# One instruction for the masked products, and an identity matmul for the own-step part, in an RWKV attention with a mixer behind it

## The chip, the cores and the metric

The kernel runs on one core of one Trainium2 chip. The metric is the device time of one execution in microseconds; of several runs the median is given. Engines are named as in the profile: PE is TensorE, DVE is VectorE, ACT is ScalarE, POOL is GpSimd, SP is SyncE, which here only issues DMAs.

## The reference

An RWKV recurrence with decay w and a bonus u for the own step, over batch 4, 8 heads, 768 steps, head size 48, and behind it a mixer over tokens (768 to 256 to 768) and channels (384 to 1536 to 384):

```python
for t in range(S):
    kt, vt, rt = (k[:, :, t], v[:, :, t], r[:, :, t])
    cur = np.einsum('bhd,bhe->bhde', u[None] * kt, vt)
    y[:, :, t] = np.einsum('bhd,bhde->bhe', rt, state + cur)
    state = w[None, :, :, None] * state + np.einsum('bhd,bhe->bhde', kt, vt)
...
h = np.maximum(xt @ w_tok1, 0.0) @ w_tok2
u = x + h.transpose(0, 2, 1)
h2 = np.maximum(u @ w_ch1, 0.0) @ w_ch2
return (u + h2).astype(np.float32)
```

Everything arrives and leaves as float32; the kernel computes most products in bf16.

## The kernel before

The 768 steps are cut into C = 6 chunks of 128, so a batch has six units (b, c), and there are 24. Inside a unit the recurrence becomes matmuls. k and r are scaled by powers of the decay (kp, rp, or wpT behind the transpose); A = kp rT, with steps that aren't earlier masked out, is multiplied with v; the state of the chunks before comes in through a matmul with S0; and the own step, u times k times r summed over a head, times v, is added. Heads lie in pairs of 64 partitions (two times 48, padded), HP = 4 pairs, and q = 0 or 1 tells which of a pair.

A unit goes through four stages, one slot apart, and each slot s runs each stage for another unit (the list STAGES in `slot`):

- `stage_p`: kp (on DVE for batch 0 but units 3 and 5, else on POOL); for batch 0 also m = k*r on POOL, for later batches rp and ku on POOL.
- `stage_a`: transposes on PE through the PSUM pool psM (four buffers, tag "m"). For batch 0 trk, trr and mT, in f32 but for trk, which ACT copies out but for trr, which DVE multiplies with wpT into rk. ACT casts v to vb.
- `stage_b`: eight matmuls give A in two PSUM tiles at_ps0 and at_ps1, one for each q; DVE multiplies each with the mask into AT0 and AT1 (bf16). For batch 0 the own step's sums come from three f32 matmuls with u_blk (ad_ps) and a copy on ACT (adg); for later batches DVE has made adg in stage_a.
- `stage_c`: y_ps sums the state's part, then A times v; kv_ps holds the state, which ACT copies out, or DVE behind chunk 2 (times wGm). DVE adds y_ps and yd, and writes x_b, the mixer's input.

yd = vb times adg is made by `own_step` on POOL: in stage_c for batch 0, in stage_b for the others.

Every engine runs its instructions in the order of the program text, so an instruction that waits holds all behind it on its engine. Batch 0 runs alone (slots 0 to 8, with one or two idle matmuls on PE behind the stages of slots 0 to 5). At the end of slots 4 to 7 POOL issues the DMAs of the mixer's weights, which also cast them to bf16: WEIGHTS_AT says which (wtok_194 in slot 4, wtok_195 in 5, wch_0 in 6, wch_1 and wch_198 in 7). At the end of slots 0 and 1 POOL makes powers, at the end of slot 3 wGm. SP issues the input loads of all units in order; that of batch 1's first unit waits, by a dependency written by hand, for the last x_b of batch 0 (`after[1, 0] = done[0, C - 1]`). From there PE's list of mixer matmuls for one batch (`up`: z_ps, `down`: h_ps) is interleaved with the slots of the next batch's attention by `merge`, which works from costs and due times written by hand.

Of the kernel before, what the change touches and what calls it, by code (L numbers as in the profile page):

```python
# [11 lines left out]
f32 = mybir.dt.float32  # L12
bf16 = mybir.dt.bfloat16
# [9 lines left out]
def kernel(  # L23
# [14 lines left out]
    B, H, S, D = r.shape  # L38
    dm = H * D
    T = 128  # L40
# [3 lines left out]
    HP = H // 2  # L44
# [8 lines left out]
    apool = ctx.enter_context(tc.tile_pool(name="apool", bufs=3))  # L53
# [3 lines left out]
    psA = ctx.enter_context(tc.tile_pool(name="psA", bufs=1, space=bass.MemoryType.PSUM))  # L57
# [12 lines left out]
    pe, dve, act, pool, sp = (InOrder(e) for e in (nc.tensor, nc.vector, nc.scalar, nc.gpsimd, nc.sync))  # L70

    def h3(t):
        return t.rearrange("p (h d) -> p h d", h=H)
# [3 lines left out]
    done = {}  # L77
# [62 lines left out]
    ident_f = const.tile([128, 128], f32, name="ident_f")  # L140
# [5 lines left out]
    mask = const.tile([128, 128], f32, name="mask")  # L146
# [99 lines left out]
    x_bs = [xpool.tile([128, C, dm], bf16, name="x_b", bufs=3) for b in range(B)]  # L246
# [63 lines left out]
    def own_step(L):  # L310
        L["yd"] = apool.tile([128, dm], f32, name="yd")
        pool.tensor_mul(h3(L["yd"]), h3(L["vb"]), L["adg"].unsqueeze(2).to_broadcast([128, H, D]))

    def stage_b(b, c):

        L = live[b, c]
        rk = L["rk"]
        if b > 0:
            own_step(L)
        at_ps = [psA.tile([128, HP, T], f32, name=f"at_ps{q}", tag=f"at{q}") for q in range(2)]  # L320
        for a in range(HP):
            for q in range(2):
                rows = slice(q * P, q * P + D)
                pe.matmul(at_ps[q][:, a, :], rk[rows, 0, a, :], rk[rows, 1, a, :], start=True, stop=True)
        L["AT"] = []
        for q in range(2):
            AT = apool.tile([128, HP, T], bf16, name=f"AT{q}")
            dve.tensor_mul(AT, at_ps[q], mask.unsqueeze(1).to_broadcast([128, HP, T]))
            L["AT"].append(AT)
        if b == 0:  # L330

            ad_ps = psM.tile([128, H], f32, name="ad_ps", tag="m")
            for j in range(3):
                pe.matmul(ad_ps, L["mT"][:, j, :], u_blk[:, j, :], start=(j == 0), stop=(j == 2))
            L["adg"] = apool.tile([128, H], f32, name="adg")
            act.copy(L["adg"], ad_ps)

    state = {}

    def stage_c(b, c):  # L340
        L = live.pop((b, c))
        rk, kp, vb = L["rk"], L["kp"], L["vb"]
        if b == 0:
            own_step(L)
        S0 = state.pop(b, None)
        y_ps = psA.tile([128, dm], f32, name="y_ps", tag="y")
        first = True
        if c > 0:
            for a in range(HP):
                pe.matmul(y_ps[:, ds(a * 2 * D, 2 * D)], rk[:, 1, a, :],  # L350
                   S0[:, a].rearrange("p q d -> p (q d)"),
                   start=first, stop=False, skip_group_check=True)
                first = False
        if c < C - 1:

            if c % G == 0:
                kv[0] = psA.tile([128, HP, 2, D], f32, name="kv_ps", tag="kv")
                if c > 0:
                    pe.matmul(kv[0].rearrange("p a q d -> p (a q d)"), ident,
                       S0.rearrange("p a q d -> p (a q d)"),  # L360
                       start=True, stop=False, skip_group_check=True)
            for a in range(HP):
                pe.matmul(kv[0][:, a].rearrange("p q d -> p (q d)"),
                   kp[:, 2 * a:2 * a + 2, :].rearrange("p q d -> p (q d)"),
                   vb[:, ds(a * 2 * D, 2 * D)],
                   start=(c == 0 and a == 0), stop=True, skip_group_check=True)
        for a in range(HP):
            for q in range(2):
                h = 2 * a + q
                pe.matmul(y_ps[:, ds(h * D, D)], L["AT"][q][:, a, :], vb[:, ds(h * D, D)],  # L370
                   start=first, stop=(h == H - 1), skip_group_check=True)
                first = False
        if c < C - 1:
            if c % G != G - 1:
                new = S0s[c % G]
                for q in range(2):
                    rows = slice(q * P, q * P + D)
                    act.copy(new[rows, :, q, :], kv[0][rows, :, q, :])
            else:
                new = apool.tile([128, HP, 2, D], bf16, name="S0")  # L380
                dve.tensor_mul(new, kv[0], wGm)
            state[b] = new
        done[b, c] = dve.tensor_add(x_bs[b][:, c, :], y_ps, L["yd"])


    mixed = {}
# [65 lines left out]

    units = [(b, c) for b in range(B) for c in range(C)]
    STAGES = ((3, stage_c), (2, stage_b), (1, stage_a), (0, stage_p))

    def slot(s, lo, hi):

        for lag, f in STAGES:
            if lo <= s - lag < hi:
                f(*units[s - lag])  # L460

# [10 lines left out]
    for s in range(C + 3):  # L472
        slot(s, 0, C)
        if s < C:
            keep_warm(WARM[1 if s < 4 else 2])
        if s < 2:
            decay_k(s + 1)
            exponents(s + 1)
        if s == 0:
            constants_1()  # L480
        if s == 3:
            constants_2()
        if 0 < s < 3:
            decay_rT(s)
        if s == 8:
            constants_3()
        if 4 < s < 8:
            decay_r(s - 5)
        load_weights(WEIGHTS_AT.get(s, ()))
        if s == C - 1:  # L490
            sp.dma_start(u_bc, u.rearrange("h d -> (h d)").partition_broadcast(128))
        if s == C + 1:
            for f in hid[:3]:
                f()
# [26 lines left out]
    def att(t, s):  # L521
        return (t, SLOT, lambda: slot(s, C, len(units)))
# [29 lines left out]
    for b in range(1, B):  # L552
# [4 lines left out]
        if b + 1 < B:  # L557
            at = [1.0, 5.0, 9.0, 13.0, 17.0, 21.5, 26.0, 30.5] if b == 1 else [0.0, 6.0, 12.0, 18.0]
# [35 lines left out]
```

## Time and profile before

| | |
|---|---|
| median of 3 runs | 186.15 us (186.05 to 186.49) |
| span of the profiled execution | 184.1 us |
| busy: PE, PEld, DVE, ACT, POOL | 165.5, 106.8, 106.0, 100.0, 93.8 us |
| chain that ended last: PE, POOL, DMA, DVE, ACT | 58%, 14%, 13%, 6%, 5% |
| DMA | 24.44 MB in 90354 packets, 133 GB/s over the span |

The span runs from the first to the last instruction of the profiled execution. What lies around it is in the runs' time and not in the span; the profiled execution has no other time of its own here, so the median stands beside the span, 2.05 us above it. PEld is the loading of weights into TensorE, which overlaps its matmuls. The chain is followed back from the last instruction to what released each one; it names what set the end, which busy time does not. All the kernel's operations go through one helper and so have one line, L68, in the profile: they are told apart by the names of their tiles.

### The profile page before, as it was taken

The numbers are of one execution on the slowest core, as the hardware profiler recorded it, in microseconds if no ns is written. First come the engines' busy times: TensorE is split into PE (matmuls) and PEld (weight loads), VectorE is DVE, ScalarE is ACT, GpSimd is POOL, SyncE is SP. The second block draws the span as 40 slices with busy tenths as digits, with TensorE's granted clock in tenths as the row PEclk, the third lists the DMA queues.
The fourth block names the chain that finished last, engine by engine and source line by source line (L and its number), as shares of the span: only waits on it lengthen the run. The fifth ranks groups of instructions, "written<-read, shape, count | busy, mean of one in ns | idle before, by whom it ended". The sixth has DMA issues, their size and how long they took to land.

```text
span 184.1 us, 3991 instructions
## 1 busy us (share of the span) xinstructions
PE 165.5 (90%) x1504; PEld 106.8 (58%) x1504; DVE 106.0 (58%) x193; ACT 100.0 (54%) x217; POOL 93.8 (51%) x113
## 2 busy tenths in 40 slices
PE   7788888893699899798999999899999999999992
PEld 2376776461367566465667666666665665656651
DVE  6465877700469999974669977996541071121121
ACT  2695565493578744404959748654645444445500
POOL 5459795002999999943597999991100000000000
PEclk9999999999699999999999999999999999999999
DMA  4999998999999998124699999233011134211212
GB/s 92 185 203 163 191 141 143 196 184 196 187 219 215 234 225 195 45 45 107 136 235 232 189 243 196 44 67 108 0 46 43 43 86 89 85 43 43 85 47 85
DMA packets 90354, 24.44 MB, mean 133 GB/s; under 512 B 83680, under 2 KB 90336, under 8 KB 90336
## 3 DMA queue, kind: packets, MB, share of 16 engines
q1 hardware_dynamic: 86368, 20.85, 54.0%
q0 software_dynamic: 3408, 3.15, 11.0%
q10 hardware_dynamic: 560, 0.20, 0.7%
q8 instruction: 12, 0.20, 0.4%
q14 instruction: 6, 0.05, 0.1%
HBM read 20.84 MB, written 4.72 MB: 139 GB/s over the span
## 4 chain that ended last, share of the span: by engine, by line
PE 58%; POOL 14%; DMA 13%; DVE 6%; ACT 5%; issue 3%; ACTq 0%; SPq 0%; DVEq 0%; POOLq 0%
PE h_ps L68 23%; PE z_ps L68 20%; DMA rt<-in_r_dram 8%; POOL ku L68 3%; POOL yd L68 3%; DMA wd<-in_w_dram 3%; PE tr_ps L68 3%; DMA uT<-u_sb 3%; PE y_ps L68 2%; PE ad_ps L68 2%; POOL rp_661 L68 2%; POOL rp_663 L68 1%; PE hT_ps L68 1%; POOL rp_665 L68 1%; DVE u_sb L68 1%
## 5 line engine op out<-in xcount | busy, mean ns | idle before, releaser
L68 ACT ACTIVATE zr<-z_ps 128x384 bf16<-128x384 f32 x96 | 44.3, 495 | 31.7 <-PE z_ps L68 31.6
L68 PE MATMUL h_ps<-wch_198,zr 128*128 128x384 bf16 x288 | 50.4, 326 | 0.2
L68 PEld LDWEIGHTS <-zr 128*128 128x128 bf16 x288 | 28.0, 98 | 18.9 <-issue 1.0
L68 DVE TENSOR_TENSOR osb<-u_sb,h_ps 128x384 f32<-128x384 bf16 x24 | 13.3, 552 | 44.5 <-PE h_ps L68 44.5
L68 ACT COPY rk<-tr_ps 128x1024 bf16<-128x1024 bf16 x18 | 18.2, 1012 | 19.2 <-PE tr_ps L68 18.7
L68 PE MATMUL z_ps<-uT,wch_0_196 128*128 128x384 bf16 x144 | 27.6, 337 | 1.1 <-DMA uT<-u_sb 1.1
L68 PE MATMUL z_ps<-uT,wch_1_197 128*128 128x384 bf16 x144 | 26.5, 326 | 0.8 <-ACT zr L68 0.6
L68 DVE TENSOR_TENSOR rku<-ku,rt 128x384 f32<-128x384 f32 x18 | 18.6, 1033 | 11.3 <-POOL ku L68 11.3
L68 POOL TENSOR_TENSOR yd<-vb,adg 128x384 f32<-128x384 bf16 x24 | 20.0, 834 | 7.3 <-DVE adg L68 6.7
L68 PEld LDWEIGHTS <-wch_0_196 128*128 128x128 bf16 x144 | 14.0, 101 | 10.4 <-issue 3.2
L68 POOL TENSOR_TENSOR ku<-kt,u_bc 128x384 f32<-128x384 f32 x18 | 20.0, 1110 | 0.0
L68 PEld LDWEIGHTS <-wch_1_197 128*128 128x128 bf16 x144 | 13.8, 98 | 10.1 <-issue 1.7
L68 DVE TENSOR_TENSOR x_b<-y_ps,yd 128x384 bf16<-128x384 f32 x24 | 13.3, 553 | 10.6 <-POOL yd L68 5.6
L68 POOL TENSOR_TENSOR kp_139<-kt,wn 128x384 bf16<-128x384 f32 x7 | 7.0, 999 | 17.2 <-DMA kt<-in_k_dram 11.5
L68 PEld LDWEIGHTS <-rk 48*128 48x128 bf16 (+1 forms) x272 | 11.4, 95 | 6.3 <-issue 3.0
L68 DVE TENSOR_TENSOR u_sb<-x_b,hT_ps 128x384 bf16<-128x384 bf16 x24 | 11.8, 547 | 1.5 <-PE hT_ps L68 1.5
L68 ACT CAST vb<-vt 128x384 bf16<-128x384 f32 x24 | 12.3, 514 | 0.0
L68 DVE TENSOR_REDUCE adg<-rku 128x8 f32<-128x384 f32 x18 | 9.9, 553 | 0.8
L68 PE MATMUL hT_ps<-h1r,wtok_195 128*128 128x384 bf16 x48 | 9.4, 326 | 0.9 <-ACT h1r L68 0.8
L68 PE MATMUL idle_ps<-warm 128*128 128x512 bf16 x20 | 7.8, 520 | 2.2 <-DVE warm L68 1.3
L68 PE MATMUL h_ps<-x_b,wtok_194 128*128 128x384 bf16 x48 | 8.9, 325 | 0.1
L68 POOL TENSOR_TENSOR rp_661<-rt,wp 128x384 bf16<-128x384 f32 x6 | 6.6, 1101 | 3.1 <-DMA rt<-in_r_dram 3.1
(318 smaller groups left out, 253.6 us busy)
## 6 DMA issues: line engine op xcount, KB each, us to landing
kt<-in_k_dram SPq DMA_DIRECT2D x24, 192.0 KB, 3.7
vt<-in_v_dram SPq DMA_DIRECT2D x24, 192.0 KB, 3.9
out_dram<-osb SPq DMA_DIRECT2D x24, 192.0 KB, 1.9
rt<-in_r_dram SPq DMA_DIRECT2D x18, 192.0 KB, 3.9
wch_198<-in_moe_w_ch_dram POOLq DMA_DIRECT2D x1, 1152.0 KB, 17.6
wch_0_196<-in_moe_w_ch_dram POOLq DMA_DIRECT2D x1, 576.0 KB, 8.9
wch_1_197<-in_moe_w_ch_dram POOLq DMA_DIRECT2D x1, 576.0 KB, 10.5
wtok_194<-in_moe_w_tok_dram POOLq DMA_DIRECT2D x1, 384.0 KB, 7.5
```

The costliest lines, as they stand in the source:

```text
L68: return lambda *args, **kw: tc.keep_in_program_order(f(*args, **kw))
```

## The change

Three things change, all in the attention.

- The two PSUM tiles at_ps0 and at_ps1 become one of the same size in total, which spans two banks, and DVE multiplies it with the mask in one instruction of 1024 elements a partition. This holds for all 24 units.
- In chunks 0 to 3 of batch 0 a last matmul, with the f32 identity as weights and yd as moving operand, adds the own-step part to y_ps, and ACT copies y_ps to x_b. In the other 20 units DVE adds as before. In batch 0 `own_step` moves from stage_c to the end of stage_b.
- In batch 0's slots the order of the stages becomes c, p, b, a, where it was c, b, a, p.

On the engines this gives the following order. POOL has yd of a unit ahead of what ends the slot (wGm and the weight DMAs) where it had it behind. DVE has kp ahead of a slot's mask product and rk. PE has one more f32 matmul in four slots, ahead of the next unit's at_ps. ACT has one more copy in these slots, ahead of adg.

```diff
         if b > 0:
             own_step(L)
-        at_ps = [psA.tile([128, HP, T], f32, name=f"at_ps{q}", tag=f"at{q}") for q in range(2)]
+        at_ps = psA.tile([128, 2, HP, T], f32, name="at_ps", tag="at")
         for a in range(HP):
             for q in range(2):
                 rows = slice(q * P, q * P + D)
-                pe.matmul(at_ps[q][:, a, :], rk[rows, 0, a, :], rk[rows, 1, a, :], start=True, stop=True)
-        L["AT"] = []
-        for q in range(2):
-            AT = apool.tile([128, HP, T], bf16, name=f"AT{q}")
-            dve.tensor_mul(AT, at_ps[q], mask.unsqueeze(1).to_broadcast([128, HP, T]))
-            L["AT"].append(AT)
+                pe.matmul(at_ps[:, q, a, :], rk[rows, 0, a, :], rk[rows, 1, a, :], start=True, stop=True)
+        AT = L["AT"] = apool.tile([128, 2 * HP, T], bf16, name="AT")
+        dve.tensor_mul(AT, at_ps.rearrange("p q a t -> p (q a) t"),
+                       mask.unsqueeze(1).to_broadcast([128, 2 * HP, T]))
         if b == 0:
...
             act.copy(L["adg"], ad_ps)
-
+            own_step(L)
+
+    BY_PE = 4
     state = {}
...
-        if b == 0:
-            own_step(L)
+        add_by_pe = b == 0 and c < BY_PE
...
-                pe.matmul(y_ps[:, ds(h * D, D)], L["AT"][q][:, a, :], vb[:, ds(h * D, D)],
-                   start=first, stop=(h == H - 1), skip_group_check=True)
+                pe.matmul(y_ps[:, ds(h * D, D)], L["AT"][:, q * HP + a, :], vb[:, ds(h * D, D)],
+                   start=first, stop=(h == H - 1 and not add_by_pe), skip_group_check=True)
                 first = False
+        if add_by_pe:
+            pe.matmul(y_ps, ident_f, L["yd"], start=False, stop=True, skip_group_check=True)
...
-        done[b, c] = dve.tensor_add(x_bs[b][:, c, :], y_ps, L["yd"])
+        if add_by_pe:
+            done[b, c] = act.copy(x_bs[b][:, c, :], y_ps)
+        else:
+            done[b, c] = dve.tensor_add(x_bs[b][:, c, :], y_ps, L["yd"])
...
+    STAGES0 = ((3, stage_c), (0, stage_p), (2, stage_b), (1, stage_a))
+
     def slot(s, lo, hi):
 
-        for lag, f in STAGES:
+        for lag, f in (STAGES if lo else STAGES0):
```

## The prediction

> **What bounds the kernel now.** I read the page first, then the chain of waits in order of time, then busy time by stretches, the timeline around 14 to 33 us, and the DMA view of single stretches. The page gives the span and the chain's shares:
>
> ```profile
> span 184.1 us, 3991 instructions
> PE 58%; POOL 14%; DMA 13%; DVE 6%; ACT 5%; issue 3%; ACTq 0%; SPq 0%; DVEq 0%; POOLq 0%
> ```
>
> One page row can't place a change that touches mostly the first 32 us, so the chain in order of time comes next (start, length, what):
>
> ```profile
> 31.19 0.56 DVE x_b L68
> ...
> 32.19 14.15 DMA rt<-in_r_dram
> 46.48 1.00 POOL rp_661 L68
> ...
> 73.23 1.28 POOL rp_663 L68
> 74.55 0.40 PE tr_ps L68 x4
> ```
>
> So there are four stages. Batch 0's attention ends with the last x_b at 31.75. The loads of batch 1 wait for that x_b by hand. Then one input row, rt of unit (1,0), is under way until 46.3. Then POOL runs until PE takes over. The stretches say which of them has slack (busy time of PE, PEld, DVE, ACT, POOL, then clock, DMA share, GB/s):
>
> ```profile
> 31.75:46.48 14.73, 10.53 (x72) 5.94 (x71) 4.19 (x10) 8.26 (x19) 1.00 (x2) 1.00 1.20 192
> 46.48:74.55 28.07, 25.18 (x285) 16.88 (x286) 23.96 (x36) 17.40 (x34) 28.07 (x29) 0.94 1.00 207
> 84.43:184.10 99.67, 95.01 (x826) 60.48 (x826) 48.82 (x86) 52.94 (x112) 36.38 (x37) 1.00 0.43 102
> ```
>
> POOL has no gap in 28.07 us: whatever moves its start at 46.48 moves all that follows. Ahead of it the DMA engines are full (share 1.20), so the start is set by bytes and by when they are queued. The last 100 us are PE's, and the change takes nothing from PE there.
>
> **The change part by part. Mask product in one instruction.** Two instructions of 512 elements become one of 1024:
>
> ```profile
> 15.36 0.68 DVE AT_346 L68
> 16.04 0.60 DVE AT_348 L68
> ...
> 16.69 0.20 PE L68 MATMUL y_ps<-vb,AT_348 128*128 128x48 bf16 x1 [0.40 <-DVE AT_348 L68]
> ```
>
> A pair takes 1.28 us. x_b, with 384 elements, takes 0.56 (above) and a half product, with 512, 0.68: 0.12 for 128 elements, so 512 more cost 0.50 and the merged one 1.18, a gain of 0.10 a unit; at worst it takes twice 0.68, a loss of 0.08. The chain holds DVE for 6% of the span, mostly ahead of 32 us; behind it I count 0.1 us of gain in all. The Trainium skill ("Perfetto Trace Analysis", Optimizing Scalar/DVE Operations) says against it that an engine that is not saturated but makes others wait should have its instructions broken up. The last row shows how little that is here: the y products alternate between the halves, so only one of eight started early, and PE then waited 0.40 for the second half. By that rule a unit would lose that one product's head start, by the row nothing.
>
> **Own-step part by TensorE, four units.** It removes four x_b additions (0.56 each) from DVE, and with them DVE's wait for POOL's yd:
>
> ```profile
> 14.03 0.82 POOL L68 TENSOR_TENSOR yd<-vb,adg 128x384 f32<-128x384 bf16 x1
> 14.88 0.56 DVE L68 TENSOR_TENSOR x_b<-y_ps,yd 128x384 bf16<-128x384 f32 x1 [1.76 <-POOL yd L68]
> ```
>
> The wait isn't gone, it changes engine: the identity matmul waits for the same yd, and behind it in PE's queue stand the next unit's at_ps, ad_ps and transposes, which ran during DVE's wait before. yd of unit 0 still stands on POOL right behind m of unit 2, so PE is held until 14.87. From there PE's work for a slot is, by the chain:
>
> ```profile
> 12.61 0.17 PE kv_ps L68 x4
> 12.78 0.20 PE y_ps L68 x8
> 12.98 0.16 PE at_ps_336 L68
> ...
> 17.29 0.21 PE at_ps_408 L68
> ...
> 17.69 0.77 PE ad_ps L68 x6
> 18.45 0.24 PE trk L68 x4
> 18.69 0.45 PE trr L68 x4
> 19.14 0.33 PE mT_ps L68 x3
> 19.46 0.23 PE idle_ps L68
> ...
> 28.56 0.21 PE at_ps_614 L68
> ...
> 29.72 0.99 PE h_ps L68 x6
> ```
>
> From at_ps to the end of idle 2.40 (17.29 to 19.69), the state's products about 0.17 (taken like kv_ps), kv_ps 0.17, y_ps 0.20: 2.94. The identity matmul (128x384, f32) is in no row. An f32 matmul is recorded twice (ad_ps x6 for three); trr, f32 with 128 columns, takes 0.45/4 = 0.11, so 384 columns 0.34, twice: 0.68. At least it is two passes at the bf16 pace (h_ps, 384 columns: 0.99/6 = 0.165), 0.33; at most each pass costs double the transposes' pace, 1.36. I take 0.68, the nearest row in type. A slot is then 3.62, and at_ps starts: unit 1 at 14.87 + 0.68 = 15.55 (at_ps_336 at 12.98 before); unit 2 at 19.37 (0.20 for a second idle matmul); unit 3 at 22.99; unit 4 at 26.78 (0.17 for a carried state). Unit 5, with no identity matmul between, at 29.72, against 28.56. Its x_b ended 3.19 behind that (31.75 - 28.56): 32.9. Batch 0 ends about 1.2 us later. DVE, eased by some 0.66 a slot, is no longer what PE waits for: a merged product that starts 0.5 behind at_ps is done 1.7 behind it, and PE needs it 2.7 behind.
>
> ScalarE gets four copies, near this one of the same size:
>
> ```profile
> L68 ACT COPY mT<-mT_ps 128x384 f32<-128x384 f32 x6 | 2.9, 478 | 1.1 <-PE mT_ps L68 1.1
> ```
>
> Each 0.48 us stands ahead of adg, which waits for ad_ps 1.1 us behind the identity matmul: hidden; if it weren't, adg and yd would come up to 0.48 later.
>
> **Order of the stages.** Putting stage_p ahead of b and a makes DVE do kp of unit 1 before rk of unit 0 (0.55 us) and kp of unit 2 before the first mask product. at_ps of unit 0 comes about 0.5 later, its mask product about 1.5; both end ahead of 14.87, when PE is held by yd anyway, so nothing. Without that hold the product's delay would count.
>
> **own_step moved to stage b.** On POOL it goes past what ends a slot: wGm and the weight DMAs. Those now stand behind a yd that waits for a fresh adg:
>
> ```profile
> 26.06 0.80 POOL L68 DMA_DIRECT2D wch_0_196<-in_moe_w_ch_dram  x1
> ...
> 27.66 0.80 POOL L68 DMA_DIRECT2D wch_1_197<-in_moe_w_ch_dram  x1
> 28.46 1.05 POOL L68 DMA_DIRECT2D wch_198<-in_moe_w_ch_dram  x1
> 30.06 0.83 POOL L68 TENSOR_TENSOR yd<-vb,adg 128x384 f32<-128x384 bf16 x1 [0.56 <-ACT adg L68]
> 31.78 0.37 SPq L68 DMA_DIRECT2D kt<-in_k_dram  x1
> ```
>
> The last yd started 1.50 behind its at_ps (30.06 - 28.56). So yd of unit 4 starts at 26.78 + 1.50 = 28.28 and ends 0.83 later: wch_0 is issued at 29.1, 3.0 later. yd of unit 5 ends at 32.05: wch_1 and wch_198 are issued at 32.05 and 32.85, 4.4 later. The inputs of batch 1 are issued at 32.9 instead of 31.78. What this costs, the DMA view of two stretches tells, 28 to 30 and 36 to 42 (queue, packets, MB, share of 16 engines):
>
> ```profile
> DMA packets 180, 0.26 MB, mean 131 GB/s; under 512 B 14, under 2 KB 179, under 8 KB 179
> ...
> q0 software_dynamic: 179, 0.25, 81.2%
> ...
> DMA packets 2226, 1.11 MB, mean 185 GB/s; under 512 B 1120, under 2 KB 2226, under 8 KB 2226
> q0 software_dynamic: 1117, 0.90, 93.9%
> q1 hardware_dynamic: 1109, 0.21, 32.1%
> ```
>
> At 28 to 30 the weight queue (q0) is already short of work, 131 against 185 GB/s: what was issued before wch_0 is running out. With wch_0 3.0 later the engines stand idle about that long, less the 0.4 us (19% of 2.0) that they lose there now. From 36 to 42 the queues get packet for packet (1117 and 1109): kt and rt crawl beside the weights and land about when the weights do. So rt and POOL's start move by the idle time: 3.0 - 0.4 = 2.6. Bounds: nothing, if rt passes the weights, and 4.4, the delay of wch_198, if it must wait for them all. wch_198 itself has cover, by its row of the page's DMA issues (us to landing last) and its first use in the timeline:
>
> ```profile
> rt<-in_r_dram SPq DMA_DIRECT2D x18, 192.0 KB, 3.9
> ...
> wch_198<-in_moe_w_ch_dram POOLq DMA_DIRECT2D x1, 1152.0 KB, 17.6
> ...
> 52.97 2.11 PE L68 MATMUL h_ps<-wch_198,zr 128*128 128x384 bf16 x12
> ```
>
> It lands at 28.46 + 17.6 = 46.1 and is used 6.9 later.
>
> **Sum.** 2.6 later, less 0.1 for the merged products: +2.5. The profiled span of 184.1 becomes 186.6; the median lies 2.05 above the span shown, and 186.15 + 2.5 = 188.6 us, 1.3% slower. With the identity matmul at 0.33, wch_0 comes 4 x 0.35 = 1.4 less late: +1.1, 187.2. At 1.36, 2.7 later: +5.2, 191.4.
>
> **The rivals. The inputs pass the weights (faster).** kt of unit (1,0) and wch_198 are issued in the same tenth of a microsecond now, where kt came 3.3 us behind before. If the largest weight's packets aren't in the rings when kt's and rt's arrive, rt stops sharing with half of the weights' bytes. It decides by whether those packets come first. If the queues shared by bytes at 185 GB/s, rt's and kt's 0.39 MB would take 4.2 us on top of the usual 3.9 to land (the row of rt just above): 32.9 + 8.1 = 41, POOL starts 5 earlier; PE, busy 25.2 of POOL's 28.1 us, lets at most some 3 of that through: 183.2. Against it: rt was issued at 32.19 and took 14.15, and in the stretch 36 to 42 the inputs got 0.21 MB of 1.11. The Trainium skill ("DMA: Bandwidth & Descriptors", Queues, rings and completion order) says an engine takes turns between rings by packets of 9 to 17 descriptors; filled to like sizes they would give the byte sharing of this rival. The equal packet counts speak against it.
>
> **DMA is full anyway (no change).** If wtok's bytes stretch until wch_0's come, no time is lost and only x_b's 1.2 us remain, hidden by the crawl: 186.2. For it: DMA share 1.20 behind 31.75. Against: 81% at 28 to 30.
>
> **The dear identity matmul**, above: 191.4. **DVE's relief comes through (faster).** If PE had room, unit 0's wait of 1.76 would shrink to the identity matmul's 0.68, and batch 0 with its weights would come 1.1 earlier: 185.0. It decides by whether PE's slot, 3.62 here, is shorter than DVE's. Against it: the chain of the first 30 us runs over PE's rows already, and yd comes no sooner.
>
> **How the numbers follow.** Main case with the cheap matmul included 0.66 (own range 187.2 to 190.5), dear matmul 0.06, full DMA 0.10, inputs pass 0.12, DVE's relief 0.06 (185.0). About 0.3% (0.56 us) is what can be told from no change. Faster 0.18; same 0.10; slower 0.72. The range leaves out the inputs passing and most of the dear matmul: 185.0 to 190.6.
>
> **What would show it.** Right: the identity matmul near 0.68 for both passes; PE, not DVE, waiting on yd near 13 to 15; at_ps of unit 5 at 29.7; wch_0 issued near 29, wch_198 near 32.9; a dip in GB/s near 31; rp of unit (1,0) on POOL near 49; equal shifts from there on. Wrong: that rp starts before 47, the last x_b before 32, or the dip is missing.

## The result, and the profile after

The changed kernel takes 188.88 us (median of 4 runs, 187.88 to 190.97) against 186.1 of the kernel before: the ratio is 1.0137, with a 95% interval of 1.009 to 1.0183. One slow run of the four is left out of the ratio, which is why it is a little below the quotient of the medians. The forecast was 188.6 and 1.3%.

The page of the profiled execution (187.88 us as a run):

```profile
span 186.1 us, 3974 instructions
PE 61%; POOL 14%; DMA 13%; ACT 4%; DVE 3%; issue 2%; ACTq 0%; SPq 0%; POOLq 0%
```

The span is 2.0 longer. By the ratio the runs are 2.55 us longer; one profile is one execution, and executions differ (25 of 27 of the kernel before had spans from 183.3 to 185.3 us). DVE's share of the chain fell from 6% to 3% and PE's rose from 58% to 61%: the wait moved from one engine to the other. The chain in order of time (start, length, what) shows where the 2.0 come in:

```profile
32.26 0.56 DVE x_b L68
...
33.26 15.23 DMA rt<-in_r_dram
48.63 1.00 POOL rp L68
...
75.38 1.28 POOL rp L68
76.70 0.40 PE tr_ps L68 x4
```

POOL starts at 48.63 where it started at 46.48, 2.15 later. From there to the tr_ps that ends POOL's part are 28.07 us, and before they were 74.55 - 46.48 = 28.07: the rest is carried along as a block.

PE's slots in batch 0, from the timeline and then the chain of waits:

```profile
14.90 0.91 PE L68 MATMUL y_ps<-yd,ident_f 128*128 128x384 f32 x2 [0.92 <-POOL yd L68]
...
18.74 0.89 PE L68 MATMUL y_ps<-yd,ident_f 128*128 128x384 f32 x2
19.56 0.40 PE L68 MATMUL at_ps<-rk 48*128 48x128 bf16 x8
...
23.16 0.40 PE L68 MATMUL at_ps<-rk 48*128 48x128 bf16 x8
```

```profile
15.82 0.33 PE at_ps L68 x8
16.15 0.77 PE ad_ps L68 x6
...
26.98 0.33 PE at_ps L68 x8
```

The identity matmul is recorded twice, and at_ps starts 0.82 behind its start (18.74 to 19.56). PE waits for yd at unit 0 and nowhere else in the four; slots follow each other without a gap. The weights on POOL and the inputs on SP, in the timeline:

```profile
28.43 0.82 POOL L68 TENSOR_TENSOR yd<-vb,adg 128x384 f32<-128x384 bf16 x1 [2.12 <-ACT adg L68]
29.20 0.80 POOL L68 DMA_DIRECT2D wch<-in_moe_w_ch_dram  x1
31.40 0.82 POOL L68 TENSOR_TENSOR yd<-vb,adg 128x384 f32<-128x384 bf16 x1 [1.40 <-ACT adg L68]
32.18 1.85 POOL L68 DMA_DIRECT2D wch<-in_moe_w_ch_dram  x2
...
32.84 0.37 SPq L68 DMA_DIRECT2D kt<-in_k_dram  x1
```

wch_0 is issued 3.1 later than before, the other two 4.5, the inputs 1.1. What the DMA engines moved from 24 to 36 us, first before the change, then behind it:

```profile
DMA packets 1892, 1.98 MB, mean 165 GB/s; under 512 B 106, under 2 KB 1889, under 8 KB 1889
```

```profile
DMA packets 1590, 1.60 MB, mean 133 GB/s; under 512 B 53, under 2 KB 1588, under 8 KB 1588
```

0.38 MB less in the same 12 us. At the 185 GB/s that they reach behind it this is 2.05 us, which is the shift of POOL's start but for 0.1. Of the 0.38, 0.30 are missing behind 30 us (1.09 MB before and 0.79 now, from 30 to 36), and most of these from 30 to 32: 37 GB/s where it was 152. This is the dip that was forecast near 31.

### The profile page after: what moved, and what is told of

It reads as the page before. It is cut to its first block, busy times and chain, and to the rows that moved or that the text cites. A ratio compares the mean times of both kernels' runs of the same rounds, so it can differ in the third digit from the quotient of the medians.

```text
span 186.1 us, 3974 instructions
## 1 busy us (share of the span) xinstructions
PE 167.7 (90%) x1512; PEld 107.3 (58%) x1512; DVE 102.1 (55%) x165; ACT 102.0 (55%) x221; POOL 93.6 (50%) x113
## 4 chain that ended last, share of the span: by engine, by line
PE 61%; POOL 14%; DMA 13%; ACT 4%; DVE 3%; issue 2%; ACTq 0%; SPq 0%; POOLq 0%
PE h_ps L68 22%; PE z_ps L68 20%; DMA rt<-in_r_dram 8%; PE y_ps L68 4%; POOL rp L68 4%; POOL yd L68 3%; POOL ku L68 3%; POOL kp L68 3%; PE tr_ps L68 3%; DMA wd<-in_w_dram 3%; PE at_ps L68 3%; DMA uT<-u_sb 3%; PE ad_ps L68 2%; PE hT_ps L68 2%; PE kv_ps L68 1%
## 5 line engine op out<-in xcount | busy, mean ns | idle before, releaser
L68 PE MATMUL z_ps<-uT,wch 128*128 128x384 bf16 x288 | 53.7, 333 | 1.9 <-DMA uT<-u_sb 1.1
L68 PE MATMUL h_ps<-wch,zr 128*128 128x384 bf16 x288 | 50.4, 326 | 0.1
L68 PEld LDWEIGHTS <-wch 128*128 128x128 bf16 x288 | 27.9, 100 | 20.7 <-issue 5.2
L68 DVE TENSOR_TENSOR AT<-at_ps,mask 128x1024 bf16<-128x1024 f32 x24 | 29.2, 1217 | 7.2 <-PE at_ps L68 7.2
L68 POOL TENSOR_TENSOR kp<-kt,wn 128x384 bf16<-128x384 f32 x20 | 20.4, 1019 | 16.9 <-PE z_ps L68 9.2
L68 POOL TENSOR_TENSOR rp<-rt,wp 128x384 bf16<-128x384 f32 x18 | 20.4, 1133 | 4.4 <-DMA rt<-in_r_dram 4.4
L68 ACT CAST S<-kv_ps 48x192 bf16<-48x192 f32 x32 | 9.9, 310 | 7.4 <-PE kv_ps L68 7.1
L68 PEld LDWEIGHTS <-wtok 128*128 128x128 bf16 x96 | 9.1, 98 | 7.5 <-issue 2.4
L68 PEld LDWEIGHTS <-kp 128*128 128x128 bf16 x176 | 10.8, 100 | 4.4 <-POOL kp L68 1.0
L68 PE MATMUL tr_ps<-ident,rp 128*128 128x128 bf16 x72 | 7.2, 224 | 6.4 <-POOL rp L68 6.3
```

The costliest lines, as they stand in the source:

```text
L68: return lambda *args, **kw: tc.keep_in_program_order(f(*args, **kw))
```

## The experiments

Three theories stood against each other. W: the loss comes in where the weights are queued later and the engines run out of bytes. I: it comes in through the later last x_b and the inputs issued behind it. P: the identity matmuls are PE time that nothing gives back.

**The weights ahead, all else as changed.**

```diff
-    WEIGHTS_AT = {4: (0,), 5: (1,), 6: (2,), 7: (3, 4)}
+    WEIGHTS_AT = {4: (0,), 5: (1,)}
...
+        if s == C:
+            load_weights((2, 3, 4))
         slot(s, 0, C)
```

> The changed kernel, but the DMAs of the channel mixer's weights (wch_0, wch_1, wch_198) are issued on POOL at the start of slot 6, ahead of the yd's that they stand behind in the change; nothing else differs, so the identity matmuls and the late last x_b stay. Theory W (the loss comes in where the weights are queued later, and the engines run out of bytes near 28 to 31): wch_0 issued near 26.4 us, rp of unit (1,0) starts on POOL at 46.5 to 47.0 as before the change (48.6 in the changed kernel), span 184.1 to 184.8, ratio to before 1.000 to 1.004. Theory I (the loss comes in through the last x_b, 1.1 later, and the inputs of batch 1 issued behind it): kt issued near 32.8 as in the changed kernel, rp starts near 47.6 or later, ratio 1.006 or more. Theory P (four identity matmuls are PE time that nothing gives back): span 186, ratio 1.011 or more.

Ratio 1.0003 (0.9971 to 1.0034), span 184.0. The timeline and the DMA view of 24 to 36:

```profile
26.69 2.57 POOL L68 DMA_DIRECT2D wch<-in_moe_w_ch_dram  x3
...
32.96 0.37 SPq L68 DMA_DIRECT2D kt<-in_k_dram  x1
...
46.43 0.99 POOL L68 TENSOR_TENSOR rp<-rt,wp 128x384 bf16<-128x384 f32 x1 [2.50 <-DMA rt<-in_r_dram]
```

```profile
DMA packets 1864, 2.01 MB, mean 167 GB/s; under 512 B 59, under 2 KB 1862, under 8 KB 1862
```

The whole loss is gone, with all four identity matmuls in place and the inputs issued at 32.96, later than in the changed kernel. From 30 to 32 the engines move 200 GB/s. I and P fall here: 1.2 us on the last x_b costs nothing, since the inputs crawl beside the weights either way. The two wtok loads are issued 1.6 and 1.4 later than before (22.21 and 25.93), so it isn't they that cost the time.

**The weights late in the kernel before.**

```diff
-    WEIGHTS_AT = {4: (0,), 5: (1,), 6: (2,), 7: (3, 4)}
+    WEIGHTS_AT = {4: (0,), 5: (1,), 7: (2,), 8: (3, 4)}
```

> The kernel before, with wch_0 issued at the end of slot 7 and wch_1 and wch_198 at the end of slot 8, behind the yd's as in the change; no other edit, so x_b and the inputs' issue stay at 31.75. Theory W: wch_0 issued near 27.7 (1.6 later than before), wch_1 and wch_198 near 31 and 31.8; rp of unit (1,0) starts near 47.7, 1.2 later, span near 185.3, ratio 1.005 to 1.009. Theory I: rp starts at 46.5, ratio within 0.003 of 1. If inputs can pass weights that are queued late: rp starts before 46, ratio under 0.998.

Ratio 1.0077 (1.0042 to 1.0111), span 185.8. The late issue alone makes a loss, and a little more of one than expected:

```profile
27.64 0.80 POOL L68 DMA_DIRECT2D wch<-in_moe_w_ch_dram  x1
...
31.15 1.84 POOL L68 DMA_DIRECT2D wch<-in_moe_w_ch_dram  x2
...
48.10 0.99 POOL L68 TENSOR_TENSOR rp<-rt,wp 128x384 bf16<-128x384 f32 x1 [3.49 <-DMA rt<-in_r_dram]
```

1.6 later than before, where 1.2 stood. The bytes of 24 to 36 (1.90 MB, 0.08 short) would give only 0.4, so here they don't carry the whole shift. Two things behind 36 us add to it. Until rt landed the inputs' queue moved 0.77 MB, against 0.70 before; kt and rt are 0.39 of that, so more of the loads issued behind rt came ahead of its last bytes. And in the last microsecond ahead of rt's landing, 47 to 48, the engines moved 0.01 MB. Why rt's last bytes come so late is not shown.

**The parts of the change, one at a time.** All but the identity matmul and ScalarE's copy:

```diff
-    BY_PE = 4
+    BY_PE = 0
```

> The changed kernel with the identity matmul and ScalarE's copy in no unit: DVE adds yd in all, the rest of the change stays (merged mask product, order of the stages, yd made in stage b). PE's slot falls from 3.6 to some 2.8 us and DVE waits for yd again. Expected: last at_ps of batch 0 near 28.0 (29.6 in the changed kernel, 28.56 before), last x_b ends near 31, wch_0 issued near 27, wch_1 near 30. Theory W: wch_0 is still some 1 us later than before, rp starts near 47.0, ratio 1.002 to 1.005. Theory I: the last x_b is 0.7 earlier, rp starts near 45.8, ratio 0.995 to 0.998.

Ratio 1.0035 (1.0003 to 1.0067), span of the profiled execution 183.6. The two don't agree in sign, for the profiled execution was the shortest of the ten; so this settles little between W and I. Against the change's 1.0137, the identity matmul with its copy brings most of the loss, and it does so by delaying yd and what stands behind it: without it wch_0 is issued at 27.25 and the engines move 1.97 MB from 24 to 36, as before. My step from wch_0's time to rp's missed here: wch_0 came 1.2 later, and rp started at 46.05, 0.4 earlier. The bytes moved told it, the time of issue did not.

yd moved alone, in the kernel before:

```diff
             act.copy(L["adg"], ad_ps)
+            own_step(L)
...
-        if b == 0:
-            own_step(L)
         S0 = state.pop(b, None)
```

> The kernel before with one part of the change: batch 0's yd made at the end of stage b, not in stage c; two mask products, DVE adds, order of the stages as before. yd is then ready ahead of m of the unit behind and DVE's wait of 1.76 at unit 0 shrinks. Expected: last x_b ends near 30.4, 1.3 earlier, the inputs of batch 1 issued with it; weights issued about when they were (wch_0 near 26, wch_198 near 28.7). Theory W: rp of unit (1,0) starts at 46.2 to 46.6, ratio within 0.003 of 1. Theory I: rp starts near 45.2, ratio 0.993.

Ratio 1.0007 (0.9968 to 1.0047), span 184.1. The chain and the timeline:

```profile
30.18 0.56 DVE x_b L68
```

```profile
46.03 0.99 POOL L68 TENSOR_TENSOR rp<-rt,wp 128x384 bf16<-128x384 f32 x1 [3.42 <-DMA rt<-in_r_dram]
```

Batch 0 ends 1.0 earlier and POOL starts 0.45 earlier; the time shows nothing, where theory I has 0.993. This speaks against I a second time, but less plainly than the first experiment did, since the last two weights are issued 0.5 later here (from 28.14), which works the other way.

The merged mask product alone, in the kernel before (the lines of at_ps and AT of the change, all else as it was):

> The kernel before with one part of the change: the merged mask product in all 24 units. Theory W: weights, yd's and the last x_b keep their times within 0.2 us, rp of unit (1,0) starts near 46.5; the merged product takes 1.22 us against 1.28 for a pair, off the path nearly everywhere: span 183.9 to 184.2, ratio within 0.003 of 1. If breaking up helped (the first half free 0.6 earlier): ratio over 1.003.

Ratio 0.9979 (0.9939 to 1.0019), span 184.2: no effect that can be told. The row of the changed kernel's page:

```profile
L68 DVE TENSOR_TENSOR AT<-at_ps,mask 128x1024 bf16<-128x1024 f32 x24 | 29.2, 1217 | 7.2 <-PE at_ps L68 7.2
```

The order of the stages alone, in the kernel before:

```diff
+    STAGES0 = ((3, stage_c), (0, stage_p), (2, stage_b), (1, stage_a))
...
-        for lag, f in STAGES:
+        for lag, f in (STAGES if lo else STAGES0):
```

> The kernel before with one part of the change: in batch 0's slots stage_p stands ahead of stages b and a. No identity matmul, two mask products, yd made in stage c. kp of units 1 and 2 now holds rk and the first mask product on DVE (some 0.5 and 1.5 us at units 0 and 1), but yd's keep their times. Theory W: the weights are issued within 0.5 us of before (wch_0 near 26, wch_198 near 28.5), so rp of unit (1,0) starts at 46.2 to 47.0 and the ratio is within 0.004 of 1, whatever the last x_b does (31.5 to 32.5).

Ratio 1.0014 (0.9976 to 1.0051): no effect that can be told. What the order does to the times of issue and to rp's start is not shown.

**A cheap identity matmul.** The changed kernel with ident in bf16, and yd in bf16 in the four units:

```diff
-            pe.matmul(y_ps, ident_f, L["yd"], start=False, stop=True, skip_group_check=True)
+            pe.matmul(y_ps, ident, L["yd"], start=False, stop=True, skip_group_check=True)
```

> The changed kernel with the identity matmul in bf16 (bf16 identity, and yd written as bf16 in the four units): one pass. Recorded once, about 0.17 us of PE's time where the f32 one took about 0.84. PE's slot falls to some 2.9 us, last at_ps of batch 0 near 27.6 (29.6 in the changed kernel), wch_0 issued near 27.3, wch_1 near 30, last x_b ends near 30.8. Theory W: wch_0 is some 1.2 later than before the change and rp of unit (1,0) starts at 46.0 to 47.3, ratio 1.000 to 1.006. Theory P (the f32 passes cost as PE time in themselves): the four times 0.67 show fully, span 183.4, ratio under 1.000.

Ratio 1.0006 (0.9975 to 1.0036), so the single pass takes back the loss, or by the interval's end at least three quarters of it. ScalarE's four copies are in this run too, so they are not what cost the time. The profiled execution, with span 185.1, lies 1.0 above the one before. Its timeline:

```profile
15.04 0.32 PE L68 MATMUL y_ps<-yd,ident 128*128 128x384 bf16 x1 [0.68 <-POOL yd L68]
15.30 0.40 PE L68 MATMUL at_ps<-rk 48*128 48x128 bf16 x8
...
19.97 1.20 POOL L68 TENSOR_TENSOR wGm<-bm,wG 128x384 f32<-128x384 f32 x1 [1.99 <-ACT wG L68]
...
26.69 0.32 PE L68 MATMUL y_ps<-yd,ident 128*128 128x384 bf16 x1 [0.39 <-POOL yd L68]
...
29.23 0.80 POOL L68 DMA_DIRECT2D wch<-in_moe_w_ch_dram  x1
...
47.32 0.99 POOL L68 TENSOR_TENSOR rp<-rt,wp 128x384 bf16<-128x384 f32 x1 [3.19 <-DMA rt<-in_r_dram]
```

The matmul is 0.26 (15.04 to 15.30), but in this execution wGm on POOL waited 2 us, the yd's behind it came late, PE stood at its fourth identity matmul, and wch_0 was issued at 29.23 as in the changed kernel. Even so rp started 1.3 earlier than there, with wch_0, wch_1 and wch_198 issued at the same times. So some 1 us of the DMA stretch is not explained by the times of issue. The inputs' queue has most of it: from 36 until rt landed it moved 0.58 MB here and 0.77 in the changed kernel, 0.19 MB or 1.0 us at 190 GB/s of loads that came ahead of rt's last bytes. How much of the recovery in the runs came by earlier weights was not seen.

**Can inputs pass the weights?** In the changed kernel they don't: from 38 to 44 the two queues go packet for packet, as they did before the change from 36 to 42.

```profile
q0 software_dynamic: 1138, 0.88, 92.8%
q1 hardware_dynamic: 1138, 0.22, 33.1%
```

In the first 3 us behind their issue they move even less: the inputs' queue has 11 packets in all of 24 to 36, with kt issued at 32.84. Equal turns don't explain that, and no run here shows what does. The rival asked what happens when the inputs are there first, so they were issued earlier:

```diff
-    after[1, 0] = done[0, C - 1]
+    after[1, 0] = done[0, 2]
```

> The changed kernel with one edit: the first input load of batch 1 waits for x_b of chunk 2 and not chunk 5, so its kt is issued near 23.9 us and not 32.8, ahead of the channel weights. If inputs share with the weights packet for packet, kt and rt of unit (1,0) have their 2048 packets some 11 us behind the start, near 37, land near 39 to 41, and the weights end where they did: rp starts on POOL near 40 to 42 and not 48.6, and the span falls by 3 to 6 (PE becomes the bound before the full 7 come through): ratio to before 0.975 to 1.000. If rt must wait for the weights to end whatever the order of issue: rp starts near 48, ratio 1.010 or more. A second risk: later wtok weights hold PE's hidden matmuls, and the last x_b of batch 0 comes after 34.

Ratio 0.9858 (0.9792 to 0.9925), span 180.8, faster than both kernels. The timeline:

```profile
25.17 0.37 SPq L68 DMA_DIRECT2D kt<-in_k_dram  x1
...
36.41 1.00 POOL L68 TENSOR_TENSOR rp<-rt,wp 128x384 bf16<-128x384 f32 x1
...
39.27 0.99 POOL L68 TENSOR_TENSOR rp<-rt,wp 128x384 bf16<-128x384 f32 x1
...
50.07 1.00 POOL L68 TENSOR_TENSOR kp<-kt,wn 128x384 bf16<-128x384 f32 x1 [2.12 <-DMA kt<-in_k_dram]
```

Two units pass the weights, and rp starts 12 earlier. Then the third unit's kt does what rt of the first did before: it crawls beside the weights until 50. The span is 5.3 shorter than the changed kernel's, less than those 12.

The same early inputs in the kernel before, with the merged product and yd moved, and no identity matmul:

> The kernel before with the merged mask product, batch 0's yd made at the end of stage b, and the first input load of batch 1 waiting for x_b of chunk 2; no identity matmul, no new order of the stages. kt of unit (1,0) is issued near 21.5 to 22, wch_0 near 26 and wch_198 near 29. If inputs share packet for packet: rp starts on POOL near 38 to 40 and not 46.5, span falls by 3 to 6, ratio 0.965 to 0.985. If rt waits for the weights whatever comes first: rp near 46, ratio within 0.003 of 1.

Ratio 0.995 (0.9918 to 0.9982), a smaller gain than in the changed kernel: the weights, issued from 26.61 on and not from 30.60, are in the way again.

```profile
26.61 0.80 POOL L68 DMA_DIRECT2D wch<-in_moe_w_ch_dram  x1
...
28.80 1.85 POOL L68 DMA_DIRECT2D wch<-in_moe_w_ch_dram  x2
...
38.50 0.99 POOL L68 TENSOR_TENSOR rp<-rt,wp 128x384 bf16<-128x384 f32 x1 [6.84 <-DMA rt<-in_r_dram]
...
49.38 1.00 POOL L68 TENSOR_TENSOR rp<-rt,wp 128x384 bf16<-128x384 f32 x1
```

One unit passes, the second waits until 49. If so, later weights should help here, though they hurt in the kernel before:

```diff
-    WEIGHTS_AT = {4: (0,), 5: (1,), 6: (2,), 7: (3, 4)}
+    WEIGHTS_AT = {4: (0,), 5: (1,), 7: (2,), 8: (3, 4)}
```

> The kernel before with the merged mask product, yd made at the end of stage b, the first input load of batch 1 waiting for x_b of chunk 2, and wch_0 issued at the end of slot 7, wch_1 and wch_198 at the end of slot 8 (behind the last yd, near 29, 30 and 31 us). Late weights cost time before because nothing else was queued; here the inputs of batch 1 are queued and should use the engines. Theory W read this way (what counts is that the engines have bytes, and which come first): kt and rt of units (1,0) and (1,1) land ahead of the weights, by 32 and 39, rp of (1,0) starts near 33 to 36, that of (1,2) near 49; span near 180, ratio 0.970 to 0.985. If late weights cost time in themselves: ratio over 0.995, the one of the kernel with the same early inputs and weights at their old places.

Ratio 0.9848 (0.9796 to 0.9901), span 182.7. The same lines that cost 0.8% in the kernel before gain 1.0% here against the run just above, with intervals that don't touch in either case. But they delay less here than there: wch_0 is issued at 27.87, 1.3 later than in the run just above, and the other two no later than in it. So what the gain goes with is wch_0 alone, and it didn't act as far as expected:

```profile
27.87 2.62 POOL L68 DMA_DIRECT2D wch<-in_moe_w_ch_dram  x3
...
34.32 0.99 POOL L68 TENSOR_TENSOR rp<-rt,wp 128x384 bf16<-128x384 f32 x1 [1.35 <-DMA rt<-in_r_dram]
47.19 0.99 POOL L68 TENSOR_TENSOR kp<-kt,wn 128x384 bf16<-128x384 f32 x1 [10.93 <-DMA kt<-in_k_dram]
```

The second unit still waited for the weights; POOL idled 10.93 us in between. Last, wch_198 alone later still, behind ku of unit (1,0):

```diff
-    WEIGHTS_AT = {4: (0,), 5: (1,), 7: (2,), 8: (3, 4)}
+    WEIGHTS_AT = {4: (0,), 5: (1,), 7: (2,), 8: (3,)}
...
-    events = [att(0.5, 6), att(4.0, 7)]
+    events = [att(0.5, 6), (0.6, 0.0, lambda: load_weights((4,))), att(4.0, 7)]
```

> The kernel just named (e10), with wch_198 alone issued still later, behind ku of unit (1,0) on POOL (near 37 us). It lands near 50 to 53, about when PE first wants it (53 in the kernel before). Theory W: units (1,1) to (1,3) get the bandwidth that wch_198 had, rp of (1,2) starts 2 to 4 us earlier than in e10; span 178 to 180.5, ratio 0.960 to 0.980. If PE stands waiting for wch_198 instead: an idle stretch of PE ahead of the first h_ps from zr, span 182 or more.

Ratio 0.9866 (0.981 to 0.9921), span 181.2: not to be told from the one before it. rp of unit (1,1) starts at 44.55, 3.9 earlier than in the last one, that of (1,2) at 50.90, 1.5 earlier and not the 2 to 4 that were expected.

## Why the prediction was right, point by point

- *The end is set by when rt of unit (1,0) lands, and POOL's part moves as a block.* Right: 28.07 us both times, and the span's 2.0 are POOL's 2.15 but for 0.15.
- *PE instead of DVE waits for yd, and only at unit 0.* Right: 0.92 us of wait, identity matmul at 14.90 (14.87 forecast).
- *The identity matmul takes 0.68.* Mis-sized: 0.82. An at_ps pass took 0.33 and not the 0.40 assumed, which gave half of that back. at_ps started at 15.75, 19.56, 23.16, 26.92 and 29.56; forecast were 15.55, 19.37, 22.99, 26.78 and 29.72. The last slot was 2.64 and not 2.94, mostly because no idle matmul runs in slot 6, where I had counted one of 0.23.
- *wch_0 at 29.1, wch_1 at 32.05, kt at 32.9.* 29.20, 32.18 and 32.84.
- *The idle time of the DMA engines is wch_0's delay of 3.0 less 0.4.* Right in kind, shown by the first two experiments; in size 2.05 by bytes and 2.15 by rp's start, where 2.6 stood. The step from wch_0's time of issue to rp's start is good to about 2 us and no better. By its rule (the delay less 0.4) rp came 0.6 earlier in the change, 1.2 earlier without the identity matmul, 1.9 earlier in the bf16 version, and 0.4 later with the weights late in the kernel before. It leaves out the wtok loads, which the change issues about 1 later too, so that they fill part of the hole (0.34 MB in the weights' queue from 28 to 30, against 0.25 before), and the loads that come ahead of rt's last bytes.
- *The sum, 2.5 later.* By the ratio 2.55, by the two profiles' spans 2.0. That the forecast agrees to a tenth is luck: the path is right, but the step that gives most of the sum is not that good.
- *Merged products: 1.18 each, 0.1 us in all.* 1.217 each, a gain of 0.06 a unit against the pair's 1.28, and nothing to be told in the time. The Trainium skill ("Perfetto Trace Analysis", Optimizing Scalar/DVE Operations) says that breaking up instructions may allow work to be completed sooner; here the two halves were not faster than the whole (0.9979 for the whole, 0.9939 to 1.0019).
- *Order of the stages costs nothing.* Nothing to be told in the time; the times of issue under it are not shown.
- *With a cheap identity matmul 187.2.* Too slow: 1.0006 of the kernel before is 186.3, and the interval's end 186.9. The profiled execution, 1.0 above the one before, would have agreed; the runs decide.
- *The rival that inputs pass the weights.* It did not happen in the change, for the reason given: packet for packet, 1138 and 1138 in 38 to 44. The Trainium skill ("DMA: Bandwidth & Descriptors", Queues, rings and completion order) says that an engine takes turns between rings packet by packet. The equal counts agree with turns; the byte sharing came only from my assumption of packets of like sizes, and 0.88 against 0.22 MB speaks against it. The rival's price, a gain of 3 us, was about right where the inputs really came first (0.9858 is 2.6).
- *The other rivals.* The dear matmul's 1.36 was 0.82. DMA was not full anyway, with 0.38 MB missing. DVE's relief did not come through: PE's slots of 3.6 to 3.8 us took its place, and the last x_b was 1.1 later.

## What to carry to other kernels

Moving a step ahead of another on an engine's queue also moves it ahead of the DMAs which that engine issues: a DMA behind an operation that waits is late by the whole wait. Where DMA is the bound, count the bytes moved in a stretch before and after; a hole in the queue is lost time, while a late issue can gain when other bytes that are wanted sooner fill the hole. A wait taken from one in-order engine and given to another is only won if nothing urgent stands behind it there.

## What the runs showed of the hardware

An f32 matmul with 384 moving columns was recorded twice and held PE 0.82 us, against 0.26 for the bf16 one in the same place. Two DMA queues with work shared by packets and not by bytes: 1138 packets each from 38 to 44, 0.88 MB against 0.22. What a wait written by hand to let the weights go first costs stands in no row of the kernel before: its rows show a slow transfer of 14.15 us. Letting the inputs start three chunks earlier took the changed kernel from 1.0137 to 0.9858; in the kernel before, with the merged product and yd moved, it took off 0.5%, and 1.5% with wch_0 issued 1.3 later as well.
